# Mirrored attention blocks written two pairs later and behind reads, two v loads moved forward, two casts moved to ScalarE

## The chip, the cores and the metric

The kernel runs on one core of a Trainium2 chip. The metric is the device time of one execution in microseconds (us). It is measured as the median of several runs; one further execution is recorded by the hardware profiler.

The engines are TensorE (PE, with its weight loads shown apart as PEld), VectorE (DVE), ScalarE (ACT), GpSimd (POOL) and SyncE (SP). In this kernel SP computes nothing. It issues nearly all transfers, one after the other, in the order in which the program names them.

## The reference

For 8 batches of 2496 rows, an attention without softmax is followed by a small mixture of experts:

```python
scores = scale * np.matmul(z, z.transpose(0, 2, 1))   # z: 8 x 2496 x 64
attn = np.maximum(scores, 0.0) ** 2
out = np.matmul(attn, v)                              # v: 8 x 2496 x 256
x = (u * out).reshape(B * S, D)
# experts: logits = x @ w_gate, argmax, the best 80 tokens of each of 8 experts
h = np.maximum(x[tok_idx] @ w1[e], 0.0)
y[tok_idx] = gate_w[tok_idx, None] * (h @ w2[e])
```

`attn` is symmetric, because the same z stands on both sides. The kernel uses that.

## The kernel before

A batch is cut into 5 chunks of 512 queries, and its keys into 20 tiles of 128. One step of the main loop is a chunk `qc` and a pair `r` of key tiles, so a chunk has 10 steps, a batch 50, and the loop 400. The whole loop is written out by hand inside `manual_schedule`, so each of PE, ACT, DVE and SP runs its instructions in exactly the order in which the code names them. `now[0]` is the number of the step.

In step i, `scores` prepares the pair of step i + 2 (`LOOK` is 2): PE forms `s` with four matmuls, ACT applies relu and square to make `a`, then `a` is split into a rounded part `ah` (a cast) and a rest `al` (a subtraction on DVE). `attend` then multiplies the pair of step i with v into `acc`, twelve matmuls. So PE needs `ah` and `al` some two steps after they are begun.

A block of keys j and queries i with i > j is the transpose of a block that was computed earlier in the same batch, so only 10 of 20 off-diagonal blocks are computed. `mirror` transposes a computed `a` on DVE in 32x32 pieces into `x_{b}_{i}_{j}`. After the last of the four tiles of a block it lets SP write `x` to DRAM (`y`, 1 MB, line 261). `mirror_back`, called at the end of each step, reads a `y` back in the right arrangement into one of four SBUF slots as `blk` (four transfers of 256 KB, line 278). It may do so from two steps after the write on, and not before a slot is free. `mirrored` then makes `ah` (ACT, line 296) and `al` (DVE) from `blk` instead of from scores.

Between these, the loop names other work of SP: the loads of the next batch's z (`zraw`), of v (`vraw`, two buffers) and u (`ut`); two small copies that make `zd`; for the chunk just finished, two transposing transfers of its result `xf` into `xq` (`chunk_store`, line 412, pair 1) and the store of `xq` (`chunk_store2`, pair 3); a block of zeros for the output (`out<-idle`, pair 5); the gates (`xs<-gall`). In the last three chunks of the program the experts' first weights (`wraw`) are loaded and split as well (`weights_ahead`).

The next batch's v is loaded and split during the last two chunks of a batch: the first two pieces are loaded at pair 8 of chunk 3, and `prep_v` (a cast on ACT, a subtraction on DVE) takes a piece at pairs 2, 4, 6, 8 and 9 of chunk 4 and lets the next load follow.

Which engine makes the cast of `ah` is fixed by a set: for diagonal blocks and for the pairs in `ON_V` of batches 1 to 7 it is DVE (line 107), else ACT (line 105).

Of the kernel before, what the change touches and what calls it, by code (L numbers as in the profile page):

```python
# [8 lines left out]
F32 = mybir.dt.float32  # L9
# [16 lines left out]
def attn_moe_kernel(ctx, tc, zT, uT, v, wg, w1, w2, out, seq, cap):  # L26
# [5 lines left out]
    nc = tc.nc  # L32
    V = nc.vector
    B, _, SP = zT.shape
# [7 lines left out]
    QT = 4  # L42
    NQ = NT // QT
# [20 lines left out]
    dram = ctx.enter_context(tc.tile_pool(name="dram", bufs=1, space=DRAM))  # L64
# [3 lines left out]
    SQ = 32  # L68
# [34 lines left out]
    def cp(eng, o, i):  # L103
        if eng is nc.scalar:
            eng.copy(out=o, in_=i)  # L105
        else:
            eng.tensor_copy(out=o, in_=i)  # L107

    def prep_zc(b, j, raw):

        zc = zpool.tile([P, CH], F32R, tag="zc", name=f"zc_{b}_{j}", bufs=NQ + 1)
        V.tensor_copy(out=zc, in_=raw)
        tt(zc[64:], raw[64:], zc[64:], ALU.subtract)
        zc_t[b, j] = zc

    def prep_zd(b, j, raw=None):

        zd = zpool.tile([P, CH], F32R, tag="zd", name=f"zd_{b}_{j}")
        if raw is None:
            nc.sync.dma_start(out=zd[64:].bitcast(F32), in_=zc_t[b, j][:64].bitcast(F32))  # L120
            nc.sync.dma_start(out=zd[:64].bitcast(F32), in_=zc_t[b, j][64:].bitcast(F32))
        else:
            nc.scalar.copy(out=zd[64:], in_=raw[64:])
            tt(zd[:64], raw[:64], zc_t[b, j][:64], ALU.subtract)
        zd_t[b, j] = zd

    def load_v(b, g):
        last = g == NQ - 1
        nf = QT - 1 if last else QT
        raw = zpool.tile([P, QT, D], F32, tag="vraw", name=f"vraw_{b}_{g}")  # L130
        r0 = g * CH
        nc.sync.dma_start(out=raw[:, :nf],
                          in_=v[b, r0:r0 + nf * P, :].rearrange("(t p) d -> p t d", p=P))
        if last:

            r1 = r0 + nf * P
            for h in range(2):
                nc.sync.dma_start(out=raw[h * 64:(h + 1) * 64, nf], in_=v[b, r1:r1 + TAIL, :])
        return raw

    def prep_v(b, g, raw, e0, e1):
        last = g == NQ - 1
        nf = QT - 1 if last else QT
        vt = vpool.tile([P, QT, 2, D], F32R, tag="vt", name=f"vt_{b}_{g}")
        cp(e0, vt[:, :nf, 0], raw[:, :nf])
        e1.tensor_tensor(out=vt[:, :nf, 1], in0=raw[:, :nf], in1=vt[:, :nf, 0], op=ALU.subtract)  # L146
        if last:

            cp(e0, vt[:, nf, 1], raw[:, nf])
            cp(e0, vt[:64, nf, 0], raw[:64, nf])  # L150
            e1.tensor_tensor(out=vt[64:, nf, 0], in0=raw[64:, nf], in1=vt[64:, nf, 1],
                             op=ALU.subtract)
        v_t[b, g] = vt
# [90 lines left out]

    half_t, y_t, blk, slot_of, free = {}, {}, {}, {}, list(range(NA))
    n32 = P // SQ
    now = [0]

    to_read = [(b, i, j, ((b * NQ + i) * NT + j * QT) // 2 - LOOK)
               for b in range(B) for i in range(NQ) for j in range(i)]  # L250
# [1 line left out]
    def mirror(b, i, j, t, a):  # L252

        if t == 0:
            half_t[b, i, j] = sqpool.tile([P, n32, QT, QT, SQ], F32, tag="x", name=f"x_{b}_{i}_{j}")
        x = half_t[b, i, j]
        V.transpose(out=x[:, :, :, t].rearrange("p n k s -> p k n s"), in_=a)  # L257
        if t < QT - 1:
            return
        y = dram.tile([n32, SQ, n32, QT * QT * SQ], F32, tag="y", name=f"y_{b}_{i}_{j}", bufs=12)  # L260
        nc.sync.dma_start(out=y.rearrange("g p h f -> (g p) (h f)"),
                          in_=x.rearrange("p h k t s -> p (h k t s)"))
        y_t[b, i, j] = y, now[0]

    def mirror_back():

        while to_read and free:
            b, i, j, use = to_read[0]
            if (b, i, j) not in y_t or y_t[b, i, j][1] + 2 > now[0] or use > now[0] + AHEAD:
                return  # L270
            to_read.pop(0)
            y = y_t.pop((b, i, j))[0]
            slot_of[b, i, j] = free.pop(0)

            m = apool.tile([P, n32, QT, QT * SQ], F32, tag=f"a{slot_of[b, i, j]}",
                           name=f"blk_{b}_{i}_{j}")
            for h in range(n32):
                nc.sync.dma_start(out=m[h * SQ:(h + 1) * SQ].rearrange("p g k f -> p g (k f)"),
                                  in_=y[:, :, h].rearrange("g p f -> p g f"))
            blk[b, i, j] = m  # L280

    def pair_tile(tag, b, qc, k, dt=F32R, bufs=3):
        return ew.tile([P, 2, CH], dt, tag=tag, name=f"{tag}_{b}_{qc}_{k}", bufs=bufs)
# [17 lines left out]
    def scores(b, qc, k):  # L301
# [16 lines left out]
        ah = pair_tile("ah", b, qc, k)  # L318
        on_v = k // QT == qc or (qc, k) in ON_V and b > 0
        cp(V if on_v else nc.scalar, ah[:, :, :nq], a[:, :, :nq])  # L320
# [44 lines left out]
    def chunk_x(b, qc):  # L365
        s = slice(0, min(CH, seq - qc * CH))
        chunk_tiles(b, qc)
        for c in range(DC):
            x_full(b, qc, c, s)
# [240 lines left out]

    NP = NT // 2

    ON_V = {(0, 8), (0, 12), (0, 16)}

    early = [(e, w, part) for e in range(2) for w in (1, 2) for part in range(2)]
    qa, qb, qz = NQ - 3, NQ - 2, NQ - 1
# [7 lines left out]
    v_raw, z_raw, w_raw = {}, {}, {}  # L624
# [68 lines left out]
    with tc.manual_schedule(engines={ET.PE, ET.Activation, ET.DVE, ET.SP}):  # L693
        prep_zc(0, 0, raw0)
        prep_zd(0, 0, raw0)
        prep_zc(0, 1, raw12[:, 0])
        scores(0, 0, 0)
        prep_v(0, 0, vraw0, nc.scalar, V)
        scores(0, 0, 2)
        v_raw[0, 1] = vraw1  # L700
        z_raw.update({(0, 2): raw12[:, 1], (0, 3): raw34[:, 0], (0, 4): raw34[:, 1]})
        constants()
        prev = None
        for i, (b, qc, r) in enumerate(steps):
            last = b == B - 1 and qc == NQ - 1
            now[0] = i
            if r == 0 and prev:
                chunk_x(*prev)
            if (b, qc) == (0, 0) and r in (0, 2, 4):
                prep_zc(0, r // 2 + 2, z_raw.pop((0, r // 2 + 2)))  # L710
            if i + LOOK < len(steps):
                nb, nqc, nr = steps[i + LOOK]
                scores(nb, nqc, 2 * nr)
            if b == 0 and qc == 0:
                if r % 2 == 0 and r < 8:
                    g = r // 2 + 1
                    prep_v(0, g, v_raw.pop((0, g)), nc.scalar, V)
                    if g + 1 < NQ:
                        v_raw[0, g + 1] = load_v(0, g + 1)
                if r == 8:  # L720
                    constants_v()
            for k in (2 * r, 2 * r + 1):
                if not last or k < NT - 3:
                    attend(b, qc, k)
            if prev:
                finished(*prev, r)

            nb, nqc = (b, qc + 1) if qc + 1 < NQ else (b + 1, 0)
            if r == 2:
                prep_u(b, qc)  # L730
            if b + 1 < B:
                if r == 1:
                    z_raw[b + 1, qc] = load_z(b + 1, qc)
                if r == 9:
                    prep_zc(b + 1, qc, z_raw.pop((b + 1, qc)))
                if qc == NQ - 2 and r == 8:
                    for g in range(2):
                        v_raw[b + 1, g] = load_v(b + 1, g)
                if qc == NQ - 1:
                    g = (r - 1) // 2 if r < 9 else 4  # L740
                    if r in (2, 4, 6, 8, 9):
                        prep_v(b + 1, g, v_raw.pop((b + 1, g)), nc.scalar, V)
                        if g + 2 < NQ:
                            v_raw[b + 1, g + 2] = load_v(b + 1, g + 2)
            if nb < B and r == 1:
                prep_zd(nb, nqc)
            if r == 5:
                zero_out(b * NQ + qc, B * NQ)
            if b == B - 1 and qc >= NQ - 3:
                weights_ahead(qc, r)  # L750
            mirror_back()
            if r == NP - 1:
                prev = b, qc

        chunk_tiles(*prev)
        for kk, c in ((3, 0), (2, 0), (3, 1), (1, 0), (2, 1), (1, 1)):
            attend(*prev, NT - kk, [c])
            if kk == 1:
                chunk_x_last(*prev, c)
        chunk_store(*prev)  # L760
        chunk_logits_last(*prev)
        gate_top(b, NQ - 1, NQ)
        gate(b, NQ - 1, NQ)
        chunk_store2(*prev)
        kb = B * BPB
        count_last(kb - 2, kb)
        blocks(ps_m, "m", gp, oh, kb - 2, kb)
# [546 lines left out]
```

## Time and profile before

| | |
|---|---|
| median of three runs | 1442.48 us (1441.51 to 1442.53) |
| the profiled execution | 1441.15 us, of which the span of instructions is 1439.4 us |
| PE, share of the span busy | 96% |
| DVE, ACT | 75%, 68% |
| 16 DMA engines of the core, queue of SP | 86.3% |
| mean granted TensorE clock | 0.991 of full speed |

Busy time of PE is counted from the start of a matmul to its modelled end, and matmuls overlap, so the 96% does not say how close PE is to its own best. What PE loses is read from the waits that the profile puts in front of single matmuls. A row of a timeline gives an instruction's start, its duration, the engine, the line, what it writes and reads, and in brackets how long its engine had been idle and what ended that.

### The profile page before, as it was taken

The numbers are of one execution on the slowest core, as the hardware profiler recorded it, in microseconds if no ns is written. First come the engines' busy times: TensorE is split into PE (matmuls) and PEld (weight loads), VectorE is DVE, ScalarE is ACT, GpSimd is POOL, SyncE is SP. The second block draws the span as 40 slices with busy tenths as digits, with TensorE's granted clock in tenths as the row PEclk, the third lists the DMA queues.
The fourth block names the chain that finished last, engine by engine and source line by source line (L and its number), as shares of the span: only waits on it lengthen the run. The fifth ranks groups of instructions, "written<-read, shape, count | busy, mean of one in ns | idle before, by whom it ended". The sixth has DMA issues, their size and how long they took to land. (4 is left out here: it accounts for less than half of the span.)

```text
span 1439.4 us, 19509 instructions
## 1 busy us (share of the span) xinstructions
PE 1385.3 (96%) x7086; PEld 1135.8 (79%) x7086; DVE 1074.9 (75%) x1530; ACT 983.1 (68%) x1263; POOL 47.5 (3%) x48
## 2 busy tenths in 40 slices
PE   8999999999999999999999999999999999999687
PEld 6788877888788887888788877888878888887466
DVE  7766788667877688677877678767887678766784
ACT  8776677767776587756676577766776667766264
POOL 0000000000000000000000000000000000000075
PEclk9999999999999999999999999999999999999899
DMA  6799978996999959997899959999598979999944
GB/s 203 207 227 223 242 198 209 239 243 157 236 247 222 251 157 216 263 213 210 232 210 237 241 156 235 240 230 259 152 233 237 240 159 238 235 231 253 207 147 134
DMA packets 300103, 311.98 MB, mean 217 GB/s; under 512 B 136184, under 2 KB 228224, under 8 KB 289760
## 3 DMA queue, kind: packets, MB, share of 16 engines
q1 hardware_dynamic: 299040, 309.11, 86.3%
q0 software_dynamic: 960, 1.56, 0.4%
q8 instruction: 57, 0.93, 0.3%
q14 instruction: 46, 0.38, 0.1%
HBM read 153.48 MB, written 126.46 MB: 194 GB/s over the span
## 5 line engine op out<-in xcount | busy, mean ns | idle before, releaser
L345 PE MATMUL acc<-al,vt 128*128 128x512 f32 (+1 forms) x1520 | 587.5, 386 | 7.3 <-DVE al L54 7.1
L343 PE MATMUL acc<-ah,vt 128*128 128x512 f32 (+1 forms) x1520 | 586.9, 386 | 6.3 <-ACT ah L296 4.0
L344 PE MATMUL acc<-ah,vt 128*128 128x512 f32 (+1 forms) x1520 | 586.0, 386 | 1.2 <-DVE vt L146 1.2
L54 DVE TENSOR_TENSOR al<-a,ah 128x1024 fp32r<-128x1024 f32 (+1 forms) x240 | 291.2, 1213 | 143.8 <-ACT ah L105 134.2
L345 PEld LDWEIGHTS acc<-al,vt 128*128 128x128 f32 x1520 | 285.7, 188 | 66.8 <-DVE al L54 14.4
L343 PEld LDWEIGHTS acc<-ah,vt 128*128 128x128 f32 x1520 | 285.8, 188 | 63.5 <-ACT ah L296 7.4
L344 PEld LDWEIGHTS acc<-ah,vt 128*128 128x128 f32 x1520 | 285.9, 188 | 55.1 <-DVE vt L146 2.0
L316 ACT ACTIVATE a<-s 128x512 f32<-128x512 f32 (+1 forms) x480 | 257.6, 588 | 83.1 <-PE s L313 73.4
L296 ACT CAST ah<-blk 128x1024 fp32r<-128x1024 f32 x160 | 166.9, 1048 | 163.0 <-DMA blk<-y 81.7
L54 DVE TENSOR_TENSOR al<-blk,ah 128x1024 fp32r<-128x1024 f32 x160 | 193.0, 1214 | 93.0 <-ACT ah L296 90.5
L317 ACT ACTIVATE a<-a 128x1024 f32<-128x1024 f32 (+1 forms) x240 | 253.0, 1054 | 7.6
L257 DVE STREAM_TRANSPOSE x<-a 128x512 f32<-128x512 f32 x320 | 207.6, 686 | 0.0
L313 PE MATMUL s<-zd,zc 128*128 128x512 f32 (+1 forms) x480 | 186.9, 389 | 0.0
L105 ACT CAST ah<-a 128x1024 fp32r<-128x1024 f32 x139 | 146.0, 1050 | 4.4
L312 PE MATMUL s<-zc,zc 128*128 128x512 f32 x320 | 131.3, 410 | 3.5 <-ACT a L316 3.4
L107 DVE CAST ah<-a 128x1024 fp32r<-128x1024 f32 (+1 forms) x101 | 68.6, 679 | 46.6 <-ACT a L317 46.6
L313 PEld LDWEIGHTS s<-zd,zc 128*128 128x128 f32 x480 | 90.4, 188 | 15.4 <-issue 0.5
L373 ACT CAST xb<-xf 128x1024 bf16<-128x1024 f32 (+1 forms) x39 | 40.1, 1027 | 57.3 <-DVE xf L362 57.2
L312 PEld LDWEIGHTS s<-zc,zc 128*128 128x128 f32 x320 | 60.1, 188 | 21.8 <-ACT a L316 11.8
L312 PE MATMUL s<-zc 128*128 128x512 f32 (+1 forms) x160 | 63.8, 399 | 7.7 <-ACT a L316 7.6
L146 DVE TENSOR_TENSOR vt<-vraw,vt 128x1024 fp32r<-128x1024 f32 (+1 forms) x40 | 46.7, 1167 | 27.8 <-ACT vt L105 27.6
L105 ACT CAST vt<-vraw 128x1024 fp32r<-128x1024 f32 (+3 forms) x56 | 44.9, 828 | 30.9 <-DMA vraw<-v 30.9
(161 smaller groups left out, 843.3 us busy)
## 6 DMA issues: line engine op xcount, KB each, us to landing
y<-x SPq DMA_DIRECT2D x80, 1024.0 KB, 5.4
blk<-y SPq DMA_DIRECT2D x320, 256.0 KB, 8.3
out<-idle SPq DMA_DIRECT2D x40, 512.0 KB, 9.3
vraw<-v SPq DMA_DIRECT2D x32, 512.0 KB, 8.4
ut<-uT SPq DMA_DIRECT2D x32, 512.0 KB, 5.4
xs<-xq SPq DMA_DIRECT2D x32, 512.0 KB, 7.6
wraw<-w SPq DMA_DIRECT2D x28, 512.0 KB, 6.1
zd<-zc SPq DMA_DIRECT2D x78, 128.0 KB, 3.5
```

The source lines that it names most:

```text
L54: V.tensor_tensor(out=o, in0=a, in1=b, op=op)
L105: eng.copy(out=o, in_=i)
L107: eng.tensor_copy(out=o, in_=i)
L257: V.transpose(out=x[:, :, :, t].rearrange("p n k s -> p k n s"), in_=a)
L296: nc.scalar.copy(out=natural(ah), in_=src)
L312: nc.tensor.matmul(s[:, :nq], zk, zc[:, :nq], start=True, stop=False)
L313: nc.tensor.matmul(s[:, :nq], zk, zd[:, :nq], start=False, stop=True)
L316: nc.scalar.activation(out=a[:, h, :nq], in_=s[:, :nq], func=AF.Relu)
L317: nc.scalar.activation(out=a[:, :, :nq], in_=a[:, :, :nq], func=AF.Square)
L343: nc.tensor.matmul(o, vt[:, t, 0, cs], ah, start=k == 0, stop=False)
L344: nc.tensor.matmul(o, vt[:, t, 1, cs], ah, start=False, stop=False)
L345: nc.tensor.matmul(o, vt[:, t, 0, cs], al, start=False, stop=False)
```

## The change

Three edits. First, `mirror` no longer names the write of `y`; it notes the block. A new function `mirror_out` names the write once two steps have passed, and it is called behind `mirror_back`, so that reads named in the same step come first. A read still waits two steps from its write's place. Second, the first two v pieces of the next batch are named at pairs 2 and 4 of chunk 3 instead of both at pair 8. Third, `ON_V` keeps only pair 8 of chunk 0: the casts of pairs 12 and 16 go from DVE to ACT in batches 1 to 7.

```diff
+    now, to_write = [0], []
...
         if t < QT - 1:
             return
-        y = dram.tile([n32, SQ, n32, QT * QT * SQ], F32, tag="y", name=f"y_{b}_{i}_{j}", bufs=12)
-        nc.sync.dma_start(out=y.rearrange("g p h f -> (g p) (h f)"),
-                          in_=x.rearrange("p h k t s -> p (h k t s)"))
-        y_t[b, i, j] = y, now[0]
+        to_write.append((now[0], b, i, j, x))
+
+    def mirror_out():
+
+        while to_write and to_write[0][0] + 2 <= now[0]:
+            _, b, i, j, x = to_write.pop(0)
+            y = dram.tile([n32, SQ, n32, QT * QT * SQ], F32, tag="y", name=f"y_{b}_{i}_{j}", bufs=12)
+            nc.sync.dma_start(out=y.rearrange("g p h f -> (g p) (h f)"),
+                              in_=x.rearrange("p h k t s -> p (h k t s)"))
+            y_t[b, i, j] = y, now[0]
...
-    ON_V = {(0, 8), (0, 12), (0, 16)}
+    ON_V = {(0, 8)}
...
-                if qc == NQ - 2 and r == 8:
-                    for g in range(2):
-                        v_raw[b + 1, g] = load_v(b + 1, g)
+                if qc == NQ - 2 and r in (2, 4):
+                    g = r // 2 - 1
+                    v_raw[b + 1, g] = load_v(b + 1, g)
...
             mirror_back()
+            mirror_out()
```

The edits move instructions on SP's queue at three kinds of place. In the rows, `y_3_1_0_4848` is the write of block (1, 0) of batch 3, with a running number at the end.

On SP, at the start of the program (batch 0, chunk 0), there stood before:

```order
L132 DMA vraw_0_2_218<-v 128x4x256
L261 DMA y_0_1_0_250<-x_0_1_0_212 128x2048
L100 DMA zraw_3_264<-zT 128x512
L120 DMA zd_0_1_266<-zc_0_1_144 64x512
L121 DMA zd_0_1_266<-zc_0_1_144 64x512
L132 DMA vraw_0_3_292<-v 128x4x256
L159 DMA ut_0_0_306<-uT 128x2x512
L261 DMA y_0_2_0_324<-x_0_2_0_286 128x2048
L278 DMA blk_0_1_0_338<-y_0_1_0_250 32x4x512 x4
L132 DMA vraw_0_4_366<-v 128x3x256
```

And there stands now:

```order
L132 DMA vraw_0_2_218<-v 128x4x256
L100 DMA zraw_3_262<-zT 128x512
L120 DMA zd_0_1_264<-zc_0_1_144 64x512
L121 DMA zd_0_1_264<-zc_0_1_144 64x512
L132 DMA vraw_0_3_290<-v 128x4x256
L159 DMA ut_0_0_304<-uT 128x2x512
L267 DMA y_0_1_0_334<-x_0_1_0_212 128x2048
L132 DMA vraw_0_4_359<-v 128x3x256
L138 DMA vraw_0_4_359<-v 64x256 x2
L236 DMA out<-idle_97 128x4x256
L284 DMA blk_0_1_0_404<-y_0_1_0_334 32x4x512 x4
```

The fourth piece of v has one write ahead of it less, and the fifth one write and one block's reads less.

On SP, at the start of a later batch (batch 3, chunk 0), there stood before:

```order
L261 DMA y_3_1_0_4848<-x_3_1_0_4814 128x2048
L412 DMA_TRANSPOSE xq_2_4_4863<-xf_2_4_4795 128x7x128 x2
L100 DMA zraw_22_4866<-zT 128x512
L120 DMA zd_3_1_4868<-zc_3_1_3946 64x512
L121 DMA zd_3_1_4868<-zc_3_1_3946 64x512
L159 DMA ut_3_0_4901<-uT 128x2x512
L261 DMA y_3_2_0_4919<-x_3_2_0_4885 128x2048
L421 DMA xs_93<-xq_2_4_4863 128x6x256
L426 DMA xs_93<-xq_2_4_4863 128x256
L278 DMA blk_3_1_0_4936<-y_3_1_0_4848 32x4x512 x4
```

And there stands now:

```order
L418 DMA_TRANSPOSE xq_2_4_4861<-xf_2_4_4795 128x7x128 x2
L100 DMA zraw_22_4864<-zT 128x512
L120 DMA zd_3_1_4866<-zc_3_1_3939 64x512
L121 DMA zd_3_1_4866<-zc_3_1_3939 64x512
L159 DMA ut_3_0_4899<-uT 128x2x512
L427 DMA xs_93<-xq_2_4_4861 128x6x256
L432 DMA xs_93<-xq_2_4_4861 128x256
L267 DMA y_3_1_0_4932<-x_3_1_0_4814 128x2048
L236 DMA out<-idle_97 128x4x256
L284 DMA blk_3_1_0_4992<-y_3_1_0_4932 32x4x512 x4
```

The first write of the batch goes behind the transposes and the small loads, and the second goes behind the first block's reads.

On SP, from chunk 3 to chunk 4 of batch 3, there stood before:

```order
L159 DMA ut_3_3_5866<-uT 128x2x512
L421 DMA xs_93<-xq_3_2_5836 128x8x256
L236 DMA out<-idle_97 128x4x256
L261 DMA y_3_4_3_6010<-x_3_4_3_5953 128x2048
L132 DMA vraw_4_0_6040<-v 128x4x256
L132 DMA vraw_4_1_6042<-v 128x4x256
L278 DMA blk_3_4_3_6061<-y_3_4_3_6010 32x4x512 x4
L412 DMA_TRANSPOSE xq_3_3_6107<-xf_3_3_6066 128x8x128 x2
L100 DMA zraw_28_6110<-zT 128x512
L120 DMA zd_4_0_6112<-zc_4_0_5145 64x512
L121 DMA zd_4_0_6112<-zc_4_0_5145 64x512
L159 DMA ut_3_4_6132<-uT 128x2x448
```

And there stands now:

```order
L132 DMA vraw_4_0_5868<-v 128x4x256
L427 DMA xs_93<-xq_3_2_5836 128x8x256
L132 DMA vraw_4_1_5914<-v 128x4x256
L236 DMA out<-idle_97 128x4x256
L267 DMA y_3_4_3_6059<-x_3_4_3_5957 128x2048
L418 DMA_TRANSPOSE xq_3_3_6102<-xf_3_3_6061 128x8x128 x2
L100 DMA zraw_28_6105<-zT 128x512
L120 DMA zd_4_0_6107<-zc_4_0_5143 64x512
L121 DMA zd_4_0_6107<-zc_4_0_5143 64x512
L284 DMA blk_3_4_3_6110<-y_3_4_3_6059 32x4x512 x4
L159 DMA ut_3_4_6132<-uT 128x2x448
L132 DMA vraw_4_2_6137<-v 128x4x256
```

The reads of the batch's last mirrored block go from ahead of the transposes and the three small transfers to behind them, and two v loads go from behind its write to ahead of it.

## Rows read from the trace of the kernel before

**Rows 1.** Waits of PE, whole span: us in total, times, longest us.

```profile
PE s L312 <- ACT a L316: 11.0, 14, 2.0
PE acc L345 <- DVE al L54: 7.1, 14, 0.8
PE acc L343 <- ACT ah L296: 4.0, 6, 1.5
```

**Rows 2.** Waits of SP's queue, same columns.

```profile
SPq L261 <- DVE x L257: 324.1, 58, 16.4
```

**Rows 3.** Timeline of SP, batch 0: the first write, the fifth v piece.

```profile
21.21 0.34 SPq L261 DMA_DIRECT2D y<-x  x1
...
32.59 0.45 SPq L132 DMA_DIRECT2D vraw<-v  x1
```

**Rows 4.** Timeline of ACT and PE, batch 0, around the stop at 40 us.

```profile
41.20 1.45 ACT L105 CAST vt<-vraw 128x768 fp32r<-128x768 f32 x3 [3.05 <-DMA vraw<-v]
...
39.20 0.39 PE L344 MATMUL acc<-ah,vt 128*128 128x512 f32 x1
39.42 0.39 PE L345 MATMUL acc<-al,vt 128*128 128x512 f32 x1
42.08 0.49 PE L343 MATMUL acc<-ah,vt 128*128 128x512 f32 x1 [2.27 <-ACT vt L105]
43.08 0.55 PE L344 MATMUL acc<-ah,vt 128*128 128x512 f32 x1 [0.50 <-DVE vt L146]
```

**Rows 5.** Busy time by window: stretch, PE, PEld, DVE, ACT, POOL, granted clock, DMA.

```profile
43.40:47.40 4.00, 4.00 (x12) 3.12 (x11) 1.66 (x3) 3.40 (x5) 0.00 (x0) 0.57 1.07 265
```

**Rows 6.** Timeline of SP, then of PE, at three changes of batch.

```profile
663.72 0.41 SPq L132 DMA_DIRECT2D vraw<-v  x1
...
171.54 0.50 PE L312 MATMUL s<-zc 128*128 128x512 f32 x1 [0.64 <-ACT a L316]
...
1003.68 0.50 PE L312 MATMUL s<-zc 128*128 128x512 f32 x1 [1.76 <-ACT a L316]
...
1170.77 0.50 PE L312 MATMUL s<-zc 128*128 128x512 f32 x1 [0.72 <-ACT a L316]
```

**Rows 7.** Timeline of ACT, batch 3, chunk 4: the casts behind late transfers.

```profile
649.88 1.05 ACT L373 CAST xb<-xf 128x1024 bf16<-128x1024 f32 x1 [1.41 <-DVE xf L362]
...
661.42 1.05 ACT L296 CAST ah<-blk 128x1024 fp32r<-128x1024 f32 x1 [4.16 <-DMA blk<-y]
...
669.10 1.05 ACT L105 CAST vt<-vraw 128x1024 fp32r<-128x1024 f32 x1 [2.88 <-DMA vraw<-v]
```

**Rows 8.** Timeline of SP, then ACT, then PE: batch 3, first mirrored block.

```profile
523.42 0.35 SPq L261 DMA_DIRECT2D y<-x  x1
...
533.79 3.43 SPq L278 DMA_DIRECT2D blk<-y  x4
...
546.49 1.99 ACT L296 CAST ah<-blk 128x1024 fp32r<-128x1024 f32 x2 [1.98 <-PE s L313]
...
547.59 0.50 PE L343 MATMUL acc<-ah,vt 128*128 128x512 f32 x1 [0.69 <-ACT ah L296]
```

**Rows 9.** Timeline of ACT, last batch, end of chunk 3.

```profile
1314.11 1.05 ACT L599 CAST w2h<-wraw 128x1024 fp32r<-128x1024 f32 x1 [4.47 <-DMA wraw<-w]
```

**Rows 10.** Timeline of SP, batch 3, chunks 3 and 4; batch 0's transposes.

```profile
645.22 0.34 SPq L261 DMA_DIRECT2D y<-x  x1
...
653.57 1.75 SPq L278 DMA_DIRECT2D blk<-y  x4
655.42 5.73 SPq L412 DMA_TRANSPOSE xq<-xf  x2
...
53.84 2.73 SPq L412 DMA_TRANSPOSE xq<-xf  x2
```

**Rows 11.** The page's group of ACT's casts, and ACT's waits for the transposes.

```profile
L105 ACT CAST ah<-a 128x1024 fp32r<-128x1024 f32 x139 | 146.0, 1050 | 4.4
...
ACT a L316 <- DVE x L257: 9.4, 14, 0.9
```

More of the change, by code (lines that the diff above doesn't have):

```diff
@@ L246, in attn_moe_kernel @@
     n32 = P // SQ
-    now = [0]
+    now, to_write = [0], []
     to_read = [(b, i, j, ((b * NQ + i) * NT + j * QT) // 2 - LOOK)
```

## Prediction

> **What bounds the kernel now.** I read the waits of PE first. PE works nearly without a break, and what it loses in the attention loop stands in a few kinds of waits: for relu on ACT before a new `s`, for `al` on DVE, and for `ah` on ACT [rows 1]. Together these are 22 us of idle time, and that is about all that a change of order can win in the loop. Each wait costs more than its idle time: the matmul at 43.08 shows 0.50 us of idle, but it starts 1.00 us behind the one at 42.08, where two undisturbed ones stand 0.22 apart (39.20 and 39.42) [rows 4]. So I take a wait as its idle time plus 0.27 us.
>
> Then I read the waits of SP's queue. SP stood 324.1 us in front of writes of `y`, 58 times, because DVE had not yet finished transposing the block, once for 16.4 us [rows 2]. In all that time SP issued nothing, and what is named behind the write came late. The question in each stage is whether somebody waited for what stood behind, and what now stands behind what else.
>
> **The change part by part.** *Batch 0, -4.6 us.* Before, SP reached the fifth piece of v at 32.59, after it had stood in front of the write issued at 21.21 [rows 3]. ACT got that piece at 41.20 after 3.05 us of waiting, and PE stopped twice: 42.08 is 2.66 behind 39.42, so 2.44 lost, and the second stop loses 0.78 [rows 4]. After it the granted clock was 0.57 in the 4.00 us that follow, between the levels of 2.4 and 1.2 GHz, and 12 matmuls took 4.00 us instead of 12 x 0.22, which is another 1.36 [rows 5]. Now the piece stands one write and four reads earlier. It must still wait for its buffer, which the third piece leaves, but about 7 us of lead against 3.05 of wait remove the stop. Sum 2.44 + 0.78 + 1.36 = 4.6; bounds 0 and 4.6.
>
> *Changes of batch, -7.6 us.* In chunk 4 ACT waits for the third v piece, in batch 3 for 2.88 us until 669.10 [rows 7], because SP issued it only at 663.72 [rows 6], behind the two transposes. These had to queue behind the reads of block (4, 3), whose write SP had stood at. The relu behind that cast comes late, and PE waits: 0.64 us at the first change, 1.76 at the sixth, 0.72 at the last of seven [rows 6]. Six such waits have 5.6 of the 11.0 us in [rows 1]; with 0.27 each and 0.4 for batch 3, where the delay is too short to be listed, that is 7.6. Now the transposes start as soon as `xf` is there, at 649.88 [rows 7], and the third piece can be issued some 5 us earlier, once its buffer is free. That is more than the 2.88 waited for here. Bounds 0 and 7.6.
>
> *First mirrored block of a batch, -6 us.* SP issued the write at 523.42 and the reads only at 533.79, since the transposes, three small transfers, a u load, the second write and a store stood between [rows 8]. ACT then stood idle for 1.98 us until 546.49. The row names PE's `s`, but those matmuls belong to a later pair; the cast reads `blk`, so I take the reads to be what came last. PE lost 0.69 of idle time on `ah` [rows 8], and then on `al`. Batches 1 to 6 have nine such waits with 4.2 us of idle time between them, out of the second and third of [rows 1]; with 0.27 each that is 6.6. Now the transposes and small loads run while DVE still transposes. The write goes at about the old time, but only a block of zeros stands between it and the reads, so these land several microseconds earlier, against 1.98 that are needed. I take 6, because a later gate on ACT (below) may leave some; bounds 0 and 6.6.
>
> *Last batch, -2.5 us.* At the end of chunk 3 ACT waited 4.47 us for an expert's weights until 1314.11 [rows 9], and PE behind it had its longest wait for `ah`, 1.5 us, and one for `al` of 0.8 [rows 1]: with 0.27 each 2.8. The weights stood behind chunk 2's blocked writes and transposes and should come some microseconds earlier. I take 2.5; bounds 0 and 5, the latter with the other two stops of this batch.
>
> *The last block of each batch, +9.8 us.* This part goes the other way. The write of block (4, 3) waits for DVE until 645.22, now as before, so nothing earlier in the queue helps it; before, its reads were next but for two v loads, and were issued when it had landed, at 653.57 [rows 10]. ACT used them at 661.42, 7.85 later, having waited 4.16 [rows 7]. Now the transposes and three small transfers stand between. The transposes cannot go before `xf` at 649.88 [rows 7]. Two of them with nothing in front took 2.73 us. With four reads in front they took 5.73, from 655.42 to 661.15, which is when those reads were in (ACT's cast follows at 661.42) [rows 10]: a transpose's issue ends only when what is ahead has landed. The small transfers take 1.9 (from 661.15 to 663.72 there is also a u load of 0.6). So the reads go at 649.88 + 2.73 + 1.9 = 654.5 at best, 0.9 later than before. If the write lands at 653.5 as before, they go at 655.4, 1.8 later. The two v loads, 1 MB, are now ahead of the write and no longer behind it; if the queue has not drained by then, a microsecond or so comes on top: 2.8. I take 1.4, between the first two as chunk 3 also begins sooner. In batch 3 the wait of 4.16 cost PE little, under 0.7, so some 3.5 us of lateness are free and are already used up: all that is added, PE loses. Seven batches x 1.4 = 9.8; bounds 7 x 0 and 7 x 2.8, or 0 and 20.
>
> The Trainium skill, DMA: Bandwidth & Descriptors, in its section on queues, rings and completion order, says that each DMA engine takes the descriptors of a ring in their order. So the v loads ahead of the write must be served first, and the rule speaks against this part; the 5.73 us of issue agree with it. By the fabric ceiling that this page gives, 435 GB/s, 1 MB is an estimated 2.4 us, and seven times that would add 17 us to the sum, if the queue were full each time.
>
> *The casts, 0.* Fourteen casts of 1.05 us each go to ACT [rows 11], 14.7 us in all, and DVE is rid of fourteen. They fall where ACT now waits for DVE to free a buffer of `a`: 14 times, 9.4 us, up to 0.9 [rows 11]. DVE, rid of a cast, frees it earlier, so nearly all of it takes the place of waiting, and PE does not wait there. Without that cover each would cost at most its 1.05; I keep +3 as the upper bound and 0 as the value, since only the gate's exponential at the end of the chunk may come some tenths later.
>
> *The other blocks, 0.* ACT waited for blocks (2, 1) and (3, 2) in most batches too, but PE did not wait behind these. They come earlier now, and that wins nothing. Writes later by two steps find their buffers: four tiles of `x` and twelve of `y`, with a block finished at most every second step.
>
> Sum: -4.6 - 7.6 - 6 - 2.5 + 9.8 = -10.9 us. The profiled execution took 1441.15, which makes 1430.2. The median of the runs is 1.3 above that execution, so I predict 1431.5.
>
> **The rivals.** *The last block costs nothing* (chance 0.16): the queue has drained when the write goes, it lands in 4 or 5 us, and the reads come as early as before. Then the gains stand alone, 20.7 us, and the median is 1421.8. For it speaks that SP stood idle in front of this write before; against it, that `xf` alone holds the transposes until 649.88.
>
> *Transfers do not come sooner* (chance 0.16): the DMA engines and not SP's order set when loads land; what SP issues earlier waits in the rings instead. Then batch 0 gives its 4.6, the other gains are small, and a part of the last block's cost remains: 1440 to 1443, in effect no change. For it speaks the queue's high load; against it, that what waited stood behind an SP that issued nothing [rows 2].
>
> *The last block takes more than all gains* (chance 0.13): its reads come 2.5 us later in every batch. PE then stops for some 3.1 us, as long as the stop in batch 0, after which the clock stood at 0.57 and cost 1.36 more [rows 4, 5]. That is 7 x (2.5 + 1.36) = 27 against 20.7, and the median is 1442.5 + 6.3 = 1448.8. It decides from 1.6 us of added lateness on if the clock falls, and from 3.0 if it does not. The Trainium skill's DMA: Bandwidth & Descriptors, with its rule on the order within a ring, describes one way to it.
>
> **How the numbers follow.** The forecast, between 1425 and 1439, has a chance of 0.55. The low end of the range, 1420, takes in the first rival; the high end, 1444, takes in the second and leaves out most of the third. What a measurement of this kernel can tell from no change is about 0.2%, 2.9 us. Faster than 1439.6 are the forecast, the first rival and a little of the second: 0.73. Within 0.2% is most of the second and the edge of the forecast: 0.14. Slower is the third: 0.13.
>
> **What the profile would show.** Right: no stop of PE in batch 0 at about 42 us and no clock at 0.57 there; SP's wait for DVE in front of writes shrunk to a fraction of 324 us; ACT's waits for `vraw` gone; the first block's cast directly behind the gate's exponential; and ACT's wait for block (4, 3) grown from some 4 to between 5 and 6 us, with PE waiting for `ah` or `al` behind it in every batch. Wrong: v pieces that are issued earlier and land no earlier, a new wait in chunk 0 between ACT and DVE, or a wait for block (4, 3) above 6.5 us with a low clock behind it.

## The result, and the profile after

The changed kernel took 1461.1 us (median of four runs, 1457.6 to 1466.7) against 1442.5 us before on the same chip: a ratio of 1.0124, 95% interval 1.0081 to 1.0168. It is slower by 18.6 us, where 1431.5 was predicted. The profiled execution, 1466.73 us, is the slowest of the four.

PE's waits, from the view of waits (what was waited for: us in all, times, longest), against [rows 1]:

```profile
PE acc L349 <- ACT ah L302: 31.8, 9, 6.0
...
PE s L318 <- ACT a L322: 5.6, 3, 2.0
PE acc L351 <- DVE al L54: 3.8, 7, 0.8
```

Two things are to be seen. Waits for relu and for `al` have halved, as hoped. The wait for `ah` of a mirrored block, 4.0 us before, is 31.8. On TensorE's timeline it stands once near the end of each of the first seven batches, in the first for 1.0 us and in the others for 4.0 to 6.0. It is block (4, 3) each time. ScalarE's timeline in batch 3, which answers to [rows 7], shows its cast:

```profile
670.73 1.04 ACT L302 CAST ah<-blk 128x1024 fp32r<-128x1024 f32 x1 [9.10 <-DMA blk<-y]
```

The prediction had named a wait above 6.5 us as a sign of being wrong; this one is 9.10. TensorE has stood for 4.45 us when the cast lets it go on:

```profile
671.83 0.74 PE L349 MATMUL acc<-ah,vt 128*128 128x448 f32 x1 [4.45 <-ACT ah L302]
```

In the 4.00 us that follow the granted clock is 0.50, the lower of the two levels, 1.2 GHz (from the view by windows: length, busy us and instructions of PE, PEld, DVE, ACT and POOL, granted clock, DMA share, GB/s):

```profile
672.30:676.30 4.00, 3.86 (x11) 2.90 (x11) 3.64 (x5) 3.97 (x6) 0.00 (x0) 0.50 0.71 145
```

Eleven matmuls of 448 columns stand in these 4.00 us; just before the stop such matmuls followed each other at 0.20 us (663.98 to 666.20 on TensorE's timeline), which makes 2.2. So in this stretch the stop costs about 1.8 us more than itself, a part of it a short wait for the first `al`. The granted clock is 0.50 behind the stop in each of batches 1 to 6.

SP's queue in that stretch, against [rows 10]:

```profile
648.41 3.25 SPq L236 DMA_DIRECT2D out<-idle  x1
651.76 1.08 SPq L267 DMA_DIRECT2D y<-x  x1
655.78 5.05 SPq L418 DMA_TRANSPOSE xq<-xf  x2
660.89 0.57 SPq L100 DMA_DIRECT2D zraw<-zT  x1
661.55 0.47 SPq L120 DMA_DIRECT2D zd<-zc  x1
662.07 0.59 SPq L121 DMA_DIRECT2D zd<-zc  x1
662.76 1.97 SPq L284 DMA_DIRECT2D blk<-y  x4
```

The transposes end at 660.83 and the write lands at 661.06; then three small loads go, and only then the reads. Before, the reads went 0.06 us after the landing.

SP's waits, against [rows 2], show where SP stands now:

```profile
SPq L284 <- DMA y<-x: 304.4, 40, 11.7
...
SPq L267 <- DVE x L257: 31.5, 19, 6.5
```

It hardly stands in front of writes for DVE any more (31.5 us against 324.1); it stands nearly as long in front of reads, for the landing of a write named right ahead of them. My first explanation began there: that SP falls behind through chunks 1 to 3, so that the write of (4, 3) is late. Its rivals were the v loads ahead of that write, the transposes ahead of its reads, and the casts.

The gains are there as well. The stop of batch 0 at 42 us is gone; matmuls follow each other at 0.22 to 0.23 us from 40.23 to 43.86. The first mirrored block is cast right behind the gate's exponential, on ScalarE's timeline, where [rows 8] had a wait of 1.98:

```profile
550.57 0.34 ACT L473 ACTIVATE ex<-d 128x160 f32<-128x160 f32 x1 [3.07 <-DVE d L54]
550.82 1.99 ACT L302 CAST ah<-blk 128x1024 fp32r<-128x1024 f32 x2
```

### The profile page after: what moved, and what is told of

Read it like the earlier page. It is cut to its first block, busy times and chain, and to the rows that moved or that the text cites. A ratio compares the mean times of both kernels' runs of the same rounds, so it can differ in the third digit from the quotient of the medians.

```text
span 1464.9 us, 19505 instructions
## 1 busy us (share of the span) xinstructions
PE 1391.4 (95%) x7085; PEld 1148.9 (78%) x7086; DVE 1070.0 (73%) x1516; ACT 999.2 (68%) x1277; POOL 45.0 (3%) x48
## 5 line engine op out<-in xcount | busy, mean ns | idle before, releaser
L349 PE MATMUL acc<-ah,vt 128*128 128x512 f32 (+1 forms) x1520 | 591.7, 389 | 31.8 <-ACT ah L302 31.8
L349 PEld LDWEIGHTS acc<-ah,vt 128*128 128x128 f32 x1520 | 289.0, 190 | 89.5 <-ACT ah L302 35.5
L351 PEld LDWEIGHTS acc<-al,vt 128*128 128x128 f32 x1520 | 289.0, 190 | 63.4 <-DVE al L54 10.4
L350 PEld LDWEIGHTS acc<-ah,vt 128*128 128x128 f32 x1520 | 289.0, 190 | 54.7 <-DVE vt L146 1.2
L105 ACT CAST ah<-a 128x1024 fp32r<-128x1024 f32 x153 | 160.6, 1050 | 4.8
L107 DVE CAST ah<-a 128x1024 fp32r<-128x1024 f32 (+1 forms) x87 | 59.1, 680 | 80.8 <-ACT a L323 80.8
L387 ACT CAST xb<-xr 128x1024 bf16<-128x1024 f32 (+1 forms) x39 | 39.9, 1024 | 20.9 <-DVE xr L54 20.4
L1059 POOL DMA_INDIRECT xg<-xs,tok x8 | 9.2, 1148 | 1394.8 <-DMA wraw<-w 1388.3
```

Of the source, the lines that this page charges most:

```text
L349: nc.tensor.matmul(o, vt[:, t, 0, cs], ah, start=k == 0, stop=False)
L350: nc.tensor.matmul(o, vt[:, t, 1, cs], ah, start=False, stop=False)
L351: nc.tensor.matmul(o, vt[:, t, 0, cs], al, start=False, stop=False)
```

## The experiments

Differences are between medians, each against the kernel before on the same chip (1440.6 to 1442.5 us).

**One part alone, and SP's standing.** *The writes only*: the changed kernel with v loads and casts undone. *The v loads only*, and *the casts only*: the kernel before with that hunk. *Writes first*: the changed kernel with its two calls exchanged, so that a write of the next block again stands between a write and its reads:

```
-            mirror_back()
             mirror_out()
+            mirror_back()
```

Expected of the writes only: 

> Only the two-pair delay of the writes and the new place of the reads stay; v loads at pair 8 and three casts on VectorE as before. Theory (SP stands at reads that are named right behind their own write, falls behind, and block (4,3) comes late): the whole loss stays, ratio 1.005 to 1.016, SP's wait of the reads for y at 250 us or more, TensorE's stop for the cast of block (4,3) 3 us or more in batches 1 to 6. Rival (the two early v loads stand ahead of the write of (4,3) on the queue and make it late): ratio 0.98 to 0.995 and that stop below 2 us. Rival (the casts on ScalarE): the same as for the v loads, below 0.995.

Expected of the v loads only: 

> The kernel before with the v loads at pairs 2 and 4 of chunk 3. Theory: no loss, 0.990 to 1.000, since ScalarE's waits for v pieces at the change of batch shrink and the reads keep their order behind other writes; SP's wait of the reads for y stays near the 48 us of before. Rival (v loads): ratio 1.008 or more, with the stop for block (4,3) at 4 us or more.

Expected of the casts only: 

> The kernel before with one cast on VectorE in place of three. Theory: no difference, 0.998 to 1.002. Rival (ScalarE, now with two more casts per chunk, is late with the casts of the mirrored blocks): 1.008 or more.

Expected of writes first: 

> The changed kernel with the two calls at the end of a step exchanged, so that the write of the next block is named ahead of the read of the one before, as in the kernel before; the two-pair delay, the v loads and the casts stay as changed. Theory: SP's wait of the reads for y falls from 304 us to below 130 us, the stop for block (4,3) falls from 4 to 6 us to below 2.5 us, and the time to 1420 to 1436 us (ratio 0.985 to 0.996), by the gains that the change had plus at most the 1.4 us a batch that the prediction gave this block. Rivals (v loads, casts, or the transposes ahead of the last block's reads, none of which this moves): still 1.008 or more.

Measured: writes only +15.0 us (ratio 1.0107, 1.0085 to 1.0129), v loads only +7.8 (1.0058, 1.0035 to 1.0080), casts only -0.7 (0.9995, 0.9980 to 1.0010), writes first +19.5 (1.0140, 1.0120 to 1.0161).

The casts cost nothing. The writes only came out as expected, with 285.0 us of SP's waits at reads; but the first explanation, from which that was expected, falls with writes first, which should have come to 0.996 at most. SP's waits there:

```profile
SPq L267 <- DVE x L257: 232.1, 49, 7.6
```

SP stands for DVE again, no longer for landings, and PE's wait is nearly as long as before the exchange:

```profile
PE acc L349 <- ACT ah L302: 29.1, 9, 4.4
```

So it does not matter for the loss what SP stands at. The writes only told less than I thought: at pair 8 the v loads go ahead of a write that is itself two pairs later, so they stood ahead of it still. The v loads alone cost something, where 1.000 at most was expected and 1.008 or more by the rival. SP's timeline of that run:

```profile
642.68 2.41 SPq L132 DMA_DIRECT2D vraw<-v  x1
645.14 4.34 SPq L236 DMA_DIRECT2D out<-idle  x1
649.58 1.08 SPq L261 DMA_DIRECT2D y<-x  x1
657.80 1.75 SPq L278 DMA_DIRECT2D blk<-y  x4
```

A store whose issue took 1.34 us in the kernel before holds SP for 4.34 while the transfers ahead are under way; the write, which DVE released at the start of the chunk's last pair (647.8), goes 1.8 us later.

**The place of the last block.** Three versions separate the v loads from the transposes. *Last at once*: the changed kernel, but block (4, 3) alone is written without delay, which names its reads ahead of the transposes and leaves the v loads ahead of its write:

```
-        while to_write and to_write[0][0] + 2 <= now[0]:
+        while to_write and (to_write[0][0] + 2 <= now[0] or to_write[0][2:4] == (NQ - 1, NQ - 2)):
```

*Last at once, v back*: that, and the v loads at pair 8, now behind the write. *V behind the write*: the changed kernel with both v loads at pair 9 of chunk 3, behind `mirror_out`; the reads stay behind the transposes. *Reads late* is the kernel before with one edit:

```
-            if (b, i, j) not in y_t or y_t[b, i, j][1] + 2 > now[0] or use > now[0] + AHEAD:
+            if (b, i, j) not in y_t or y_t[b, i, j][1] + (4 if i + j == 2 * NQ - 3 else 2) > now[0] or use > now[0] + AHEAD:
```

Expected of last at once: 

> The changed kernel, but block (4,3) is written without the two-pair delay, so that its reads stand ahead of the transposes of chunk 3; the two v loads still stand ahead of its write. Theory now (two lateness terms: the v loads ahead of the write hold it 1.6 to 2 us, the transposes and three small loads ahead of the reads 1.7 us): the second goes, block (4,3) is cast about 2 to 3 us later than before instead of 4.8, TensorE's stop is 1 to 3 us, the time 1436 to 1450 us (ratio 0.997 to 1.006). Rival (all writes, two pairs later, crowd the queue and the place of the last block is not the point): stop still above 4 us, ratio 1.008 or more.

Expected of last at once, v back: 

> As the run of block (4,3) written at once, and with the v loads back at pair 8, which is behind its write: the queue's order from the write of (4,3) to its reads is that of before, all other writes are two pairs later. Theory: both terms go, the stop for (4,3) is below 1 us as before, the gains stay, 1418 to 1432 us (ratio 0.984 to 0.994). Rival (the delay of the other writes): 1.005 or more.

Expected of v behind the write: 

> The changed kernel with both v loads named behind the write of (4,3), whose delay stays, so that its reads stay behind the transposes. Theory: the write is issued when it was before and lands 1.5 to 2 us sooner than in the changed kernel; the reads still wait for the transposes, 1.7 us, so the cast is 1.5 to 2.5 us later than before, the stop 1 to 2.5 us, the time 1432 to 1446 us (ratio 0.993 to 1.004). If only the v loads counted: stop below 1 us and 1420 to 1432 us. If only the transposes counted: stop above 4 us and 1455 us or more.

Expected of reads late: 

> The kernel before with one thing changed: the reads of block (4,3) are named two pairs later, which puts them behind the transposes and three small loads of chunk 3. Theory: 1.7 to 1.9 us later reads in each of eight batches, with the stop for this block 1.3 to 2 us and the lower clock behind it, 1450 to 1462 us (ratio 1.005 to 1.015). Rival (the lateness is hidden, as the transposes were waiting for the same queue anyway): 0.998 to 1.002.

Measured: last at once -9.8 us (ratio 0.9934, 0.9912 to 0.9955), last at once with v back -17.6 (1423.0 us, 0.9897, 0.9864 to 0.9929), v behind the write +13.3 (1.0100, 1.0076 to 1.0124), reads late +34.1 (1.0239, 1.0207 to 1.0271). The first came out better than expected, the second as expected, the third worse, and the fourth worse by far than the 1.7 us a batch that I had still given the transposes.

Reads late shows why. SP's timeline:

```profile
658.74 0.34 SPq L261 DMA_DIRECT2D y<-x  x1
659.12 1.48 SPq L132 DMA_DIRECT2D vraw<-v  x2
663.65 5.66 SPq L412 DMA_TRANSPOSE xq<-xf  x2
...
671.20 1.98 SPq L278 DMA_DIRECT2D blk<-y  x4
```

The write lands at 666.56, as early after its issue as before. The transposes end at 669.31, when the second v load lands (669.52 by the queue's completion events). After three small loads the reads go at 671.20, 4.64 us behind the landing. In last at once, with the v loads ahead of the write, the reads have only the write to wait for:

```profile
639.47 1.36 SPq L267 DMA_DIRECT2D y<-x  x1
648.37 1.75 SPq L284 DMA_DIRECT2D blk<-y  x4
650.21 4.92 SPq L418 DMA_TRANSPOSE xq<-xf  x2
```

and with the v loads back behind the write nothing is left of the stop:

```profile
PE acc L349 <- ACT ah L302: 2.5, 3, 1.2
```

**The v loads out of the way.** *V in chunk 2*: the changed kernel with the two loads at pairs 4 and 6 of chunk 2. *V in chunk 2, last at once*: that and the edit above. *Writes first, last at once, v back*: the fastest version with the calls exchanged too.

```
-                if qc == NQ - 2 and r in (2, 4):
-                    g = r // 2 - 1
+                if qc == NQ - 3 and r in (4, 6):
+                    g = r // 2 - 2
```

Expected of v in chunk 2: 

> The changed kernel with the first two v loads at pairs 4 and 6 of chunk 2, one chunk sooner, so that neither stands between the end of chunk 2 and the reads of block (4,3); the reads stay behind the transposes. Theory (the transposes end only with the landing of all that is ahead of them, the v loads above all, and three small loads of 1.8 us follow): with only the write ahead of them the reads come 1.8 us after its landing, the cast 1.5 to 2.5 us later than before, stop 1 to 2.5 us, 1432 to 1444 us (ratio 0.994 to 1.003). Rival (the place behind the transposes costs over 4 us whatever else is on the queue): stop above 3.5 us, 1450 us or more.

Expected of v in chunk 2, last at once: 

> The same v loads in chunk 2, and block (4,3) written at once, so that its reads stand ahead of the transposes. Theory: neither term is left, 1417 to 1430 us, within 5 us of the run with the v loads at pair 8 behind the write; stop for (4,3) below 1 us. Rival (a MB more in chunk 2 makes the other blocks late): 1434 us or more, with ScalarE's wait for blocks in chunk 3 above 60 us.

Expected of writes first, last at once, v back: 

> Block (4,3) written at once, v loads at pair 8, and besides each step's writes named ahead of its reads, so that SP does not stand at each read for its own write's landing. Theory (SP's standing costs nothing by itself): within 5 us of the run that has the first two edits alone, 1418 to 1430 us, with SP's wait of the reads for y well below 130 us. Rival (the standing does cost, once the last block is out of the way): 1410 to 1417 us.

Measured: +13.7 us (ratio 1.0090, 1.0063 to 1.0116), -7.1 (0.9948, 0.9929 to 0.9966), -15.1 (0.9888, 0.9861 to 0.9915). The first is the rival's number: the place behind the transposes is dear with the v loads gone too. The second, 1433.7 us, misses its theory (1430 at most) and just misses its rival (1434 or more); ScalarE's waits for blocks, 57.4 us in the whole program, are longer than in last at once with v back (26.4). The third came out as expected. SP's timeline of v in chunk 2:

```profile
640.85 1.95 SPq L284 DMA_DIRECT2D blk<-y  x4
...
648.52 0.34 SPq L267 DMA_DIRECT2D y<-x  x1
654.19 3.07 SPq L418 DMA_TRANSPOSE xq<-xf  x2
657.32 0.88 SPq L100 DMA_DIRECT2D zraw<-zT  x1
...
659.49 1.99 SPq L284 DMA_DIRECT2D blk<-y  x4
```

The write goes when it did before, but takes 10.6 us to land in the mean of batches 1 to 6, against 7.8 before. The reads of block (4, 2), four transfers of 256 KB that stand ahead of it on the queue, went only 7.7 us ahead of it here (640.85), and 9.1 us ahead in the kernel before, whose write went at 645.22 [rows 10] (the second row is the store of 1.34 us named above):

```profile
636.17 1.98 SPq L278 DMA_DIRECT2D blk<-y  x4
...
639.19 1.34 SPq L236 DMA_DIRECT2D out<-idle  x1
```

So more of the queue was still to be served when the write came. The third version says again that SP's standing costs nothing: its median lies within 3 us of the one that stands.

**All runs side by side.** Block (4, 3), mean of batches 1 to 6, in us from the first accumulating matmul of chunk 4; landings are the queue's completion events, the rest the timelines of SP and ScalarE:

| kernel | first read of (4, 2) issued | write issued | landed | first read, after landing | cast | run against before |
|---|---|---|---|---|---|---|
| before | -11.1 | -2.2 | 5.5 | 0.1 | 14.1 | 0 |
| changed | -10.3 | 0.2 | 9.1 | 2.2 | 19.4 | +18.6 |
| writes only | -12.0 | -1.9 | 8.7 | 2.0 | 18.8 | +15.0 |
| v loads only | -11.1 | -1.1 | 7.9 | 0.1 | 15.4 | +7.8 |
| writes first | -11.1 | -1.0 | 8.1 | 2.1 | 18.4 | +19.5 |
| v behind the write | -12.0 | -2.2 | 4.7 | 5.0 | 18.1 | +13.3 |
| v in chunk 2 | -8.3 | -2.2 | 8.4 | 1.9 | 18.5 | +13.7 |
| reads late | -11.1 | -2.2 | 5.5 | 5.1 | 18.8 | +34.1 |
| last at once | -11.4 | -1.3 | 7.7 | 0.1 | 15.3 | -9.8 |
| v in chunk 2, last at once | -8.3 | -2.2 | 8.1 | 0.1 | 15.6 | -7.1 |
| last at once, v back | -12.2 | -2.2 | 4.2 | 0.1 | 12.9 | -17.6 |
| writes first, last, v back | -11.1 | -2.2 | 5.5 | 0.1 | 14.0 | -15.1 |

Wherever the reads stand behind the transposes, the cast comes at 18 or later; wherever they stand ahead, at 15.6 at the latest. Moving this one place is worth 28.4 us with the v loads ahead of the write (+18.6 against -9.8), 30.9 with them behind it, 20.8 with them in chunk 2, and 34.1 alone, on the kernel before.

The table also says what sets the landing. In the seven kernels that have no v load between the reads of (4, 2) and the write of (4, 3), the write lands 16.4 to 16.7 us after the first of those reads was issued, although its own issue is 6.1 to 10.0 us behind it. In the five that have both v loads between, it lands 19.0 to 20.7 us after. So here the landing follows from what is ahead on the queue, and a later issue of the write alone does not move it. Putting the v loads into chunk 2 only moves the price: these reads then go at -8.3, where they go at -12.0 and -12.2 with the v loads behind the write.

## Why the prediction was wrong

*Batch 0, -4.6*: right. The stop is gone, and batch 0, from its first accumulating matmul to that of batch 1, went from 168.0 to 163.5 us in last at once with v back; in the changed kernel it took 165.7, as its own block (4, 3) took some back.

*First mirrored block of a batch, -6*: right in kind and too small. The figures are means of batches 1 to 6, from the first accumulating matmul of a chunk to that of the next. Chunks 0 and 1, where this block is awaited and used, are together 1.8 us shorter than before in last at once with v back, and 2.0 in the changed kernel itself. That is 11 to 12 us for six batches, above the bound of 6.6.

*Changes of batch, -7.6*: shown in part only. Chunk 4, counted to the next batch, is 1.3 us shorter than before in last at once with v back, which makes 7.7, and PE's waits for relu are down from the 11.0 us of [rows 1]. But in writes first, last at once, v back it is 0.2 shorter, and these waits are as long as before. The two rows, in this order:

```profile
PE s L318 <- ACT a L322: 4.0, 2, 2.2
...
PE s L318 <- ACT a L322: 11.1, 8, 2.5
```

The term rested on a third v piece issued some 5 us earlier. Against the first accumulating matmul of chunk 4 it goes at 16.4 us before, at 13.8 in the changed kernel, and at 15.1 and 16.2 in the two just named. Of the four it is clearly earlier only where the transposes stand ahead of the reads, so this gain and the last block's loss hang on the same order. In the changed kernel ScalarE's waits for v pieces are no longer listed, perhaps because the cast of (4, 3) ahead of them is late; the fastest version still has 20.1 us of them against 30.9.

*Last batch, -2.5*: not seen. From its first accumulating matmul to the last it takes 169.4 us before and in the fastest version alike, and 172.2 in the changed kernel.

*Casts, 0*: right, by the run of the casts only.

*The last block of each batch, +9.8*: here it failed. The step said that the write "waits for DVE until 645.22, now as before, so nothing earlier in the queue helps it", took its landing as at most a microsecond later, put the reads 1.8 us behind it, and took 1.4 for both. The reads stand 2.2 us behind the landing, nearly the working's 1.8. The landing is what it missed: 3.6 us later. By the table some 0.9 of that is the reads of (4, 2), which go later, and some 2.7 the v loads behind them; the write's own issue, 2.4 us later behind a store that the transfers ahead hold back (3.25 us of issue above), does not add to it. So what is earlier in the queue does set this landing, which the step denied. The cast is 5.3 us late instead of 1.4, and the conversion that the step used, "all that is added, PE loses", held in kind: reads late casts the block 4.65 us later and takes 34.1 us, 4.3 for each of eight batches.

The step also treated the v loads and the transposes as two small terms beside each other. The transposes tie them together: as [rows 10] let one see, their issue ends with the landing of all that is ahead, and so whatever stands ahead of them, on either side of the write, stands ahead of the reads. With v ahead of the write the landing is late; with v behind it, the transposes are late (4.7 and 5.0 in the table, against 9.1 and 2.2), and the cast comes at 18.1 and 19.4. The Trainium skill's rule on the order within a ring (DMA: Bandwidth & Descriptors, on queues, rings and completion order) pointed there. The runs agree: in the run of the v loads only the reads of (4, 2) go when they did before, and the write lands 2.4 us later (7.9 against 5.5), as much as the prediction's estimate from the page's fabric ceiling. The 17 us that were made of it are not shown: the cast comes only 1.3 us later there, and the v loads cost 7.8 us, about 1.1 a batch, in that run and again between the two versions that write at once.

The sum, from the runs: gains of 17.6 against a predicted 20.7, and a loss of 36.2 (18.6 and 17.6) against 9.8. The lengths of batches above are from the profiled execution of last at once with v back, 1418.1 us, the fastest of its four, so they add up to some 23 us and not to the 17.6 of the medians. Of the loss, 28 us is the place behind the transposes and 8 the v loads if the place is mended first, and 31 and 5 in the other order. The third rival, at 0.13, had the mechanism, the lower clock included (0.50 for 4.00 us, where it took 0.57), with half the lateness.

Not settled: why the reads of (4, 2) go 1.2 us later in the changed kernel than in last at once (-10.3 and -11.4), which has the same transfers ahead of them in the same order. In batch 3 SP's timelines agree from the transposes of chunk 0 to the first write, 4.2 to 11.4 us after the batch's first accumulating matmul. From there each read waits for the landing of its write and the next write stands behind the read, and the changed kernel's lag grows from 0.5 us at the first block's reads to 2.1 at the third's. Why its transfers land later to begin with I did not find. In one batch, the third, last at once is itself as late, its reads of (4, 2) at -8.1, and stops for 4.3 us.

## What to carry to other kernels

When a step is named later on a queue, find every instruction that it drops behind, and ask of each when its issue ends; if one of them waits for all that is ahead, the step inherits every transfer there, and the terms do not add but follow each other. Price the landing from what is ahead on the queue, and not from the write's own issue. A hand-off by a write and its reads is as late as the worst place on its way, so a general delay can be kept and the one block with a deadline excepted from it: here that alone turned +18.6 us into -9.8, and with the v loads back behind the write into -17.6.

## What the hardware showed that I had not expected

SP standing for 304 us at reads for landings, or 232 at writes for DVE, made no difference to the time (+18.6 and +19.5 us), and the fastest version stands for 315 us at reads. In the seven kernels without v loads between, the landing of a 1 MB write followed the transfers ahead of it to within 0.3 us in the mean, while its own issue moved by 4 us against them. Two DMA transposes held SP until what was ahead of them had landed, to within some 0.2 us (660.83 and 661.06, 669.31 and 669.52). The issue of a plain store took 3.25 and 4.34 us where both v loads had just been issued ahead of it, against 1.34 in the kernel before and 0.97 in reads late, where they stand behind it: a busy queue showed as a long issue and not as a wait of SP.
